# The order of loads and of seven hidden products in the spectral stage, and where the right sums are made, in a two-layer FNet and spatial-shift MLP kernel

## The chip, the cores and the metric

The kernel runs on one core of one Trainium2 chip. TensorE multiplies, VectorE (DVE) and ScalarE (ACT) prepare its operands and take its results, GpSimd (POOL) does little, and SyncE (SP) issues nearly all DMA transfers. Each engine works off its own list of instructions in order; a semaphore joins them where one needs the other's result. The metric is the time of one execution on the device in microseconds (us), lower is better.

## The reference, cut to what matters

Two layers, each made of a Fourier mixing stage A and a spatial-shift MLP stage B, with S = 2048 rows and D = 512 columns, F = 1376, all float32.

```python
def A(x):                       # FNet mixing, on the normed x
    a = x @ dft_hid_re.T        # hidden DFT
    b = x @ dft_hid_im.T
    return dft_seq_re @ a - dft_seq_im @ b      # DFT along the sequence, real part
def B(x):
    h = gelu(layernorm(x) @ w1)
    g = [the four column quarters of h, shifted by +1, -1, +2, -2 rows]
    x1 = x + concat(g) @ w2
    return x1 + gelu(layernorm(x1) @ w3) @ w4
for layer in range(2):
    x = x + A(layernorm(x))
    x = x + B(layernorm(x))
```

## The kernel before, in words

**Three products for one.** Every float32 operand is split into a high part (a copy rounded to the type fp32r, made on ACT) and a low part (the difference, made on DVE). `mm3` (L328 to L330) then multiplies high by high, high by low and low by high. So before TensorE can use a block of data, ACT must have made its high part and, behind it, DVE its low part.

**The spectral stage of layer 1.** It works through four column blocks c of the sequence DFT. For each block there is an x-phase (`x_phase`) and a y-phase (`y_phase`). An x-phase has eight steps k of two half-steps each. The even half-step 2k multiplies a "plain" block into the PSUM banks psc and psb: 12 products of 512 columns. The odd half-step 2k+1 multiplies the "one" block, a difference of the plain block's two halves, into psa: 6 products. A y-phase also has eight steps, with blocks "by1" (into psc and psd) and "by0" (into psb and psa), 12 products each; these blocks are sums of two loaded pieces.

**The seven forms.** In the x-phases of blocks 1, 2 and 3 the hidden DFT of the block before is done as well. It is a product of 2×2 sub-blocks, made by a scheme of seven products ("forms") in place of eight. `hid7` issues form n: 24 products of 256 columns into the PSUM bank psd0 or psd1, by turns. The left factor is one of seven sums of the earlier block (`forms`); its high part goes into one of two tiles, `hf[n % 2]` (`form_high`, on ACT, L475), its low part to its place (`form_low`, on DVE, L479). The right factors, seven right sums of the hidden DFT matrix, are the same for all blocks. They lie in DRAM (`hsd`, seven tiles of two halves), already split, and are loaded as needed. `hid7_out` adds a form's PSUM bank into the result tiles (DVE, `add`, L552). The tuple `HAT7` says ahead of which half-step each form stands; the dictionary `late` says at which half-step each left sum, high part and low part is issued.

**Loads.** All blocks of the stage are one list of `pieces` of 512 KB. `issue_dma` issues them in the order of the list, each as soon as one of the raw buffers is free: there are four, and in these phases two more ("wide"), six in all. A raw buffer of a DFT block is free once its parts are made; that of a form's half once TensorE has used it. If the next piece finds no buffer, no later one is issued. `prefetch` makes the parts of coming blocks, up to the four tiles of the ring. A DMA shows as `raw<-in_ws` for a DFT block and as `rawr<-hsd` for half of a form's right factor.

**Where the right sums come from.** They are made once, in layer 0, during the last pair of MLP blocks (`by_pairs` with `next_too`). There TensorE runs over the MLP's hidden blocks in products of 512 columns. At 26 points of that loop a function `one()` pops one item off the list `bg` and issues it; an item is other background work (preparing the next layer's blocks). `hs_forms` makes the right sums in four quarters; `hs_quarter` gives each quarter's work: load m, load r (the imaginary and the real part of a piece of the hidden DFT matrix, 256 KB each), four sums on DVE, and for each of the seven results a high part (ACT), a low part (DVE) and a store to `hsd`. In the program before, a quarter's work is seven items, some of them merged by `do_both`, and stands over 23 of the points, each behind the point's own item. The MLP's own weights, `w3b` (1792 KB) and `w4r` (512 KB), are loaded by the same queue, SP's. The tiles `rest` hold the sums of the MLP's branches; DVE (`add`, L552) and ACT (L1303) take PSUM banks through them.

What else touches the x-phases of layer 1: `w4_sums` at half-steps 10 and 11 (four sums of 256 columns on DVE, a high and a low part), `y_stats` (the statistics of a normalization, BATCH_NORM on DVE), and loads of result tiles by `rows`.

Of the kernel before, what the change touches and what calls it, by code (L numbers as in the profile page):

```python
# [8 lines left out]
F32 = mybir.dt.float32  # L9
# [9 lines left out]
NP = NT // 2  # L19
# [21 lines left out]
HAT7 = (3, 5, 7, 9, 10, 12, 14)  # L41
# [3 lines left out]
def spectral_mlp_kernel(ctx: ExitStack, tc: tile.TileContext, x, ws, hs, w1, w2, w34, out):  # L45
# [123 lines left out]
    def form_items(step):  # L169
        for h in range(7):  # L170
            if HAT7[h] == step:
                for j in range(2):
                    item("form", piece(hsd[h][j]), dest=hsd)
                    y_pieces.add(len(pieces) - 1)

    for layer in range(LAYERS):
        for c in range(NC):
            if layer == 0 and c == 0:
                for k in range(NP):
                    item("plain", piece(ws[c, k][:, 2:4]))  # L180
                    item("plain", piece(ws[c, k][:, 0:2]))
                continue
            for k in range(NP):
                if c and layer:
                    form_items(2 * k)
                elif c:
# [5 lines left out]
                if c and layer:  # L192
                    y_pieces.add(p)
                    form_items(2 * k + 1)
# [364 lines left out]
    def x_phase(c, hook, seven=False, tiles=0):  # L559
# [13 lines left out]
        for k in range(NP):  # L573
# [15 lines left out]
            mm_half(PB, ax[k][:, 1], s[:, 1], first, last)  # L589
            if last:  # L590
# [4 lines left out]
            form_steps(2 * k + 1)  # L595
# [4 lines left out]
            mm_half(PA, ax[k][:, 0], s[:, 0], first, last)  # L600
        for i in range(2):
            nc.scalar.copy(re0s[:, i], PA[i])

    def y_phase(c, hook, tiles=0):
# [32 lines left out]
        if tiles:  # L637
            for i, f in (
                (0, form_sum(im1s, im1s, re1s)),
                (0, form_sum(im1s, im1s, X1, ALU.add)),  # L640
                (1, lambda: form_high(0)),
                (1, form_sum(s3[1], a11f, a21f)),
                (2, lambda: form_low(0)),
                (2, form_sum(re1s, re1s, t[:, 0:2], ALU.add)),
                (3, form_sum(re0s, re0s, t[:, 0:2], ALU.add)),
                (3, form_sum(re0s, re0s, t[:, 2:4], ALU.add)),
                (4, lambda: form_high(1)),
                (4, form_sum(s2[1], a22f, s3[1])),
                (4, form_sum(a21f, a21f, a22f, ALU.add)),
                (4, lambda: form_low(1)),  # L650
                (5, lambda: form_high(2)),
                (5, form_sum(a11f, a12f, s2[1])),
                (6, lambda: form_low(2)),
                (7, lambda: form_high(3)),
                (8, lambda: form_low(3)),
                (8, lambda: form_high(4)),
                (9, lambda: form_low(4)),
                (10, lambda: form_high(5)),
                (11, lambda: form_low(5)),
                (12, lambda: form_high(6)),  # L660
                (13, lambda: form_low(6)),
# [180 lines left out]
    def by_pairs(layer, zs, xin, dst):  # L842
# [261 lines left out]
        def do_both(f, g):  # L1104
            return lambda: (f(), g())
# [81 lines left out]
        def hs_quarter(m, r, fp, places):  # L1187
# [948 lines left out]
```

## Time and profile before

| | us |
|---|---|
| median of 3 runs | 1500.86 (1498.94 to 1501.42) |
| profiled execution, its own time | 1500.71 |
| its span, first to last instruction | 1498.6 |
| TensorE busy | 1436.8 |
| VectorE busy | 1205.8 |
| ScalarE busy | 733.4 |
| TensorE waits for low parts at L479 (s, reL, imL) | 39.2 |
| mean granted TensorE clock | 0.987 |

The span leaves out 2.1 us that lie around it. A row of a wait list reads: who waits, for whom and which line, total us, times, longest. A row of the timeline reads: start, length, engine, line, operation, output <- input, shapes, and in brackets how long the engine had idled and what released it; PE's products are pipelined, so the distance from one start to the next is the cost of one, not its length. A granted clock of 0.50 means that TensorE ran at half speed there.

### The profile page before, as it was taken

The page shows a single profiled execution, that of the slowest core. Times are in us where ns is not written, and L with a number is a line of the kernel's source. Part 1 is how long each engine was busy: PE and PEld are TensorE (multiplying, and loading weights), DVE is VectorE, ACT ScalarE, POOL GpSimd, SP SyncE. Part 2 cuts the span into 40 slices and gives each one's busy share as a digit, 9 for nine tenths or more (in the row PEclk, how much of TensorE's full clock was granted, in tenths as well). Part 3 has the DMA queues.
Part 4 walks back from the last instruction along what each step waited for, and adds up shares of the span by engine and source line. Part 5 has one row for each costly group of instructions (what it writes and reads, how often), then busy time and mean ns, then how long its engine had stood idle before and what let it go on. Part 6 is the DMA issues. An engine that isn't in the chain of part 4 may idle for free.

```text
span 1498.6 us, 18501 instructions
## 1 busy us (share of the span) xinstructions
PE 1436.8 (96%) x6681; PEld 1200.9 (80%) x6681; DVE 1205.8 (80%) x1725; ACT 733.4 (49%) x1020; POOL 74.5 (5%) x105
## 2 busy tenths in 40 slices
PE   9999999999999999988999789889879999999999
PEld 7888888888888888866788678678768888889887
DVE  7986988989878886667899679769759887897676
ACT  5664454545566554344464234334325676454342
POOL 2100000000011000000000000000000011000000
PEclk9999999999999999989999989999989999999999
DMA  7866658478537679666655666666667637587864
GB/s 250 275 207 230 190 169 278 156 256 278 180 115 216 233 260 346 234 235 208 233 197 181 197 192 216 196 200 222 197 219 221 195 118 245 172 256 224 322 188 171
DMA packets 145628, 325.24 MB, mean 217 GB/s; under 512 B 10624, under 2 KB 61568, under 8 KB 142848
## 3 DMA queue, kind: packets, MB, share of 16 engines
q1 hardware_dynamic: 145536, 324.05, 65.5%
q8 instruction: 53, 0.87, 0.2%
q14 instruction: 39, 0.32, 0.1%
HBM read 262.41 MB, written 61.60 MB: 216 GB/s over the span
## 4 chain that ended last, share of the span: by engine, by line
PE 81%; DVE 9%; DMA 5%; ACT 3%; issue 2%; SPq 0%; POOL 0%; DVEq 0%; ACTq 0%; POOLq 0%
PE psd L330 9%; PE psd L328 8%; PE psd L329 8%; PE psa L330 7%; PE psa L329 7%; PE psa L328 7%; PE psb L330 6%; PE psb L329 6%; PE psb L328 6%; PE psc L329 6%; PE psc L330 6%; PE psc L328 6%; DMA raw<-in_ws 3%; DVE ring L285 2%; DMA hsd<-hp 1%
## 5 line engine op out<-in xcount | busy, mean ns | idle before, releaser
L264 ACT CAST ring<-raw 128x1024 fp32r<-128x1024 f32 x103 | 107.9, 1051 | 108.6 <-DMA raw<-in_ws 48.5
L285 DVE TENSOR_TENSOR ring<-raw,ring 128x1024 fp32r<-128x1024 f32 x102 | 124.1, 1219 | 41.6 <-ACT ring L264 41.5
L271 ACT CAST ring<-ring0f 128x1024 fp32r<-128x1024 f32 x28 | 29.5, 1052 | 69.1 <-DVE ring0f L270 69.1
L368 POOL TENSOR_TENSOR rs<-ve,mhalf 128x4 f32<-128x4 f32 x16 | 24.0, 1501 | 786.2 <-DVE nm L367 786.2
L285 DVE TENSOR_TENSOR ring<-ring1f,ring 128x512 fp32r<-128x512 f32 (+1 forms) x56 | 53.3, 951 | 5.2 <-ACT ring L267 5.1
L328 PE MATMUL psd<-rawr,hf 128*128 128x256 f32 x168 | 53.1, 316 | 3.6 <-ACT hf L475 3.6
L329 PE MATMUL psd<-rawr,hf 128*128 128x256 f32 x168 | 52.2, 310 | 0.0
L285 DVE TENSOR_TENSOR ring<-ring3f,ring 128x1024 fp32r<-128x1024 f32 (+1 forms) x50 | 49.2, 984 | 2.8 <-ACT ring L267 2.4
L328 PE MATMUL psd<-ring,ay 128*128 128x512 f32 x126 | 49.2, 391 | 1.9 <-DVE tmp L552 1.9
L347 POOL TENSOR_TENSOR rs<-ve,mhalf 128x2 f32<-128x2 f32 (+2 forms) x33 | 29.4, 889 | 434.2 <-DVE nb L346 415.2
L376 ACT ACTIVATE tmp<-xs,nb,rs 128x512 f32<-128x512 f32 x56 | 43.3, 810 | 14.5 <-POOL nb L348 13.0
L329 PE MATMUL psb<-ring,ay 128*128 128x512 f32 x128 | 49.9, 390 | 0.0
L328 PE MATMUL psb<-ring,ay 128*128 128x512 f32 x128 | 49.8, 389 | 0.0
L328 PE MATMUL psc<-ring,ay 128*128 128x512 f32 x128 | 49.8, 389 | 0.0
L330 PE MATMUL psb<-ring,ay 128*128 128x512 f32 x128 | 49.8, 389 | 0.0
L330 PE MATMUL psc<-ring,ay 128*128 128x512 f32 x128 | 49.8, 389 | 0.0
L329 PE MATMUL psc<-ring,ay 128*128 128x512 f32 x128 | 49.8, 389 | 0.0
L330 PE MATMUL psd<-ring,ay 128*128 128x512 f32 x126 | 49.0, 389 | 0.0
L328 PE MATMUL psa<-ring,ay 128*128 128x512 f32 x126 | 49.0, 389 | 0.0
L330 PE MATMUL psa<-ring,ay 128*128 128x512 f32 x126 | 49.0, 389 | 0.0
L329 PE MATMUL psa<-ring,ay 128*128 128x512 f32 x126 | 49.0, 389 | 0.0
L329 PE MATMUL psd<-ring,ay 128*128 128x512 f32 x126 | 49.0, 389 | 0.0
(898 smaller groups left out, 4766.9 us busy)
## 6 DMA issues: line engine op xcount, KB each, us to landing
raw<-in_ws SPq DMA_DIRECT2D x183, 512.0 KB, 5.0
w4r<-w4d SPq DMA_DIRECT2D x44, 512.0 KB, 4.7
rawr<-hsd SPq DMA_DIRECT2D x42, 512.0 KB, 4.1
w3b<-w3d SPq DMA_DIRECT2D x10, 1792.0 KB, 9.4
raw<-in_hs SPq DMA_DIRECT2D x32, 512.0 KB, 3.9
w3d<-w3b SPq DMA_DIRECT2D x5, 1792.0 KB, 6.9
hsd<-hp SPq DMA_DIRECT2D x28, 256.0 KB, 2.8
x1d<-tmp SPq DMA_DIRECT2D x12, 512.0 KB, 6.8
```

The costliest lines, as they stand in the source:

```text
L264: nc.scalar.copy(dest[:, a:b, 0], r[0][:, a:b])
L271: nc.scalar.copy(dest[:, :, 0], lo)
L285: nc.vector.tensor_tensor(lo, src, hi.bitcast(F32), op=ALU.subtract)
L328: nc.tensor.matmul(o, lh, rh, start=first, stop=False, skip_group_check=more)
L329: nc.tensor.matmul(o, lh, rl, start=False, stop=False, skip_group_check=more)
L330: nc.tensor.matmul(o, ll, rh, start=False, stop=last, skip_group_check=more)
L347: nc.gpsimd.tensor_tensor(rs[:, :n], ve[:, :n], mhalf[:, 0, :n], op=ALU.pow)
L368: nc.gpsimd.tensor_tensor(rs, ve, mhalf[:, :, :2], op=ALU.pow)
L376: nc.scalar.activation(o, s, AF.Identity, bias=mr[2], scale=mr[1])
```

## The change

Nothing is computed differently; the same products, sums and loads stand in another order. Four things are changed.

1. **Loads of an x-phase and its y-phase.** For blocks 1 to 3 of layer 1, a new function `ahead_pieces` lists all pieces of both phases with a due time in half-steps: a DFT block of x at 2k − 4.5, a form's halves one half-step before its place, a piece of y at 16 + 2k − 3.5. The list is sorted by due time and issued in that order. The items (the order in which blocks are used) take their pieces from it by name. All of these pieces may use the wide buffers.
2. **Places of the forms.** `HAT7` goes from (3, 5, 7, 9, 10, 12, 14) to (5, 10, 11, 12, 13, 14, 15), and the `late` list of sums, highs and lows is dealt out anew. The x-phase's last copies of PSUM banks stand behind the form of half-step 15, and `form_outs(2 * NP)` behind the last half-step issues what outs are left.
3. **Small moves in the x-phases.** `w4_sums` goes from half-steps 10 and 11 to 13 and 15, and a load of `pairs[1]` from 5 to 7.
4. **The right sums.** A quarter has five parts: the four sums; results 3, 4, 2; results 0, 1; result 6; result 5. They stand at 20 points, five for each quarter. In a point, the highs stand ahead of the point's own item and the lows and stores behind it. The next quarter's loads of m and r stand behind the fourth and the fifth point. The tiles lie at other places, so that the loads do not overwrite what is still in use.

```diff
-HAT7 = (3, 5, 7, 9, 10, 12, 14)
+XLEAD, YLEAD = 4.5, 3.5
+HAT7 = (5, 10, 11, 12, 13, 14, 15)
...
-    def form_items(step):
+    def ahead_pieces(c):
+        order = [(2 * k - XLEAD, 0, (k,), ws[c, k][:, 2:4]) for k in range(NP)]
+        order += [(t - 1, j, (h, j), hsd[h][j]) for h, t in enumerate(HAT7) for j in range(2)]
+        for k in range(NP):
+            order += [(2 * NP + 2 * k - YLEAD, i, (k, "y", i), ws[c, k][:, 2 - 2 * i : 4 - 2 * i]) for i in range(2)]
+        order.sort(key=lambda o: o[:2])
+        ids = {name: piece(src) for _, _, name, src in order}
+        y_pieces.update(ids.values())
+        return ids
+
+    def form_items(step, ids):
         for h in range(7):
             if HAT7[h] == step:
                 for j in range(2):
-                    item("form", piece(hsd[h][j]), dest=hsd)
-                    y_pieces.add(len(pieces) - 1)
+                    item("form", ids[h, j], dest=hsd)
 
     for layer in range(LAYERS):
         for c in range(NC):
...
+            if c and layer:
+                ids = ahead_pieces(c)
+                for k in range(NP):
+                    form_items(2 * k, ids)
+                    item("plain", ids[(k,)])
+                    form_items(2 * k + 1, ids)
+                    item("one", ids[(k,)], span=(0, 1))
+                for k, kind in y_order():
+                    item(kind, ids[k, "y", 0], ids[k, "y", 1])
+                continue
             for k in range(NP):
-                if c and layer:
-                    form_items(2 * k)
-                elif c:
+                if c:
                     for h in range(NP):
                         if HAT[h] == k:
                             item("plain", piece(hs[HORDER[h % 4]]))
                 p = piece(ws[c, k][:, 2:4])
                 item("plain", p)
-                if c and layer:
-                    y_pieces.add(p)
...
             form_outs(2 * k)
             mm_half(PC, ax[k][:, 2], s[:, 0], first, last)
             mm_half(PB, ax[k][:, 1], s[:, 1], first, last)
+            form_steps(2 * k + 1)
             if last:
                 for i in range(2):
                     nc.scalar.copy(im1s[:, i], PC[i])
                 for i in range(2):
                     nc.scalar.copy(re1s[:, i], PB[i])
-            form_steps(2 * k + 1)
             s = stream()
             run_late(2 * k + 1)
             hook(2 * k + 1)
             form_outs(2 * k + 1)
             mm_half(PA, ax[k][:, 0], s[:, 0], first, last)
+        form_outs(2 * NP)
         for i in range(2):
             nc.scalar.copy(re0s[:, i], PA[i])
 
...
             for i, f in (
                 (0, form_sum(im1s, im1s, re1s)),
-                (0, form_sum(im1s, im1s, X1, ALU.add)),
-                (1, lambda: form_high(0)),
-                (1, form_sum(s3[1], a11f, a21f)),
-                (2, lambda: form_low(0)),
-                (2, form_sum(re1s, re1s, t[:, 0:2], ALU.add)),
...
-                (8, lambda: form_low(3)),
-                (8, lambda: form_high(4)),
-                (9, lambda: form_low(4)),
-                (10, lambda: form_high(5)),
-                (11, lambda: form_low(5)),
-                (12, lambda: form_high(6)),
-                (13, lambda: form_low(6)),
+                (1, form_sum(im1s, im1s, X1, ALU.add)),
+                (2, lambda: form_high(0)),
+                (2, form_sum(s3[1], a11f, a21f)),
...
+                (6, form_sum(re0s, re0s, t[:, 2:4], ALU.add)),
+                (7, lambda: form_high(1)),
+                (7, form_sum(s2[1], a22f, s3[1])),
+                (8, lambda: form_high(2)),
+                (8, form_sum(a21f, a21f, a22f, ALU.add)),
+                (8, lambda: form_low(1)),
+                (9, form_sum(a11f, a12f, s2[1])),
+                (9, lambda: form_low(2)),
+                (10, lambda: form_high(3)),
+                (11, lambda: form_low(3)),
+                (11, lambda: form_high(4)),
+                (12, lambda: form_low(4)),
+                (12, lambda: form_high(5)),
+                (13, lambda: form_low(5)),
+                (13, lambda: form_high(6)),
+                (14, lambda: form_low(6)),
...
                 d, v = n // 2, slice(n % 2, n % 2 + 1)
-                m, r = (at(f"hs{i}{n}", STG + word, 1, CH, dtype=F32) for i, word in (("m", CH), ("r", 0)))
-                fp = [both(f"hp{i}{n}", RAWS + i * CH + CH, 1, 2, DH) for i in range(3)]
+                m, r = (at(f"hs{i}{n}", RAWS + (1 + i) * CH, 1, CH, dtype=F32) for i in range(2))
+                fp = [both(f"hp{i}{n}", word, 1, 2, DH) for i, word in enumerate((RAWS + 3 * CH, STG, STG + CH))]
                 steps += hs_quarter(m, r, fp, [(t[d][:, v], hs[(1, d)][:, v], hs[(0, d)][:, v]) for t in hsd])
             return steps
...
             def load_r():
                 nc.sync.dma_start(r, places[0][2])
 
-            def out(i, n, src=None):
-                t, src = fp[i][0], raw[i] if src is None else src
-                act(t[:, :, 0], src)
-                nc.vector.tensor_tensor(t[:, :, 1], src, t[:, :, 0].bitcast(F32), op=ALU.subtract)
-                nc.sync.dma_start(places[n][0].rearrange("p i (l w) -> p i l w", l=2), t.bitcast(F32))
-
             def sums():
-                add(raw[0], b22, b12, ALU.subtract)
                 add(raw[1], b12, b11, ALU.subtract)
-                out(0, 4)
-
-            def more_sums():
-                add(raw[2], b22, raw[1], ALU.subtract)
-                add(b12, raw[2], b21, ALU.subtract)
-                out(1, 3)
-
-            return [
-                load_m,
-                load_r,
-                sums,
-                more_sums,
-                lambda: out(2, 2),
-                lambda: (out(0, 0, b11), out(1, 1, b12)),
-                lambda: (out(2, 6, b21), out(0, 5, b22)),
+                add(raw[2], b22, b12, ALU.subtract)
+                add(raw[0], b22, raw[1], ALU.subtract)
+                add(b12, raw[0], b21, ALU.subtract)
+
+            def outs(*which):
+                which = [(i, n, raw[i] if src is None else src) for i, n, src in which]
+
+                def highs_():
+                    for i, _, src in which:
+                        act(fp[i][0][:, :, 0], src)
+
+                def lows_():
+                    for i, n, src in which:
+                        t = fp[i][0]
+                        nc.vector.tensor_tensor(t[:, :, 1], src, t[:, :, 0].bitcast(F32), op=ALU.subtract)
+                        nc.sync.dma_start(places[n][0].rearrange("p i (l w) -> p i l w", l=2), t.bitcast(F32))
+
+                return highs_, lows_
+
+            nothing = lambda: None
+            parts = [
+                (nothing, sums),
+                outs((1, 3, None), (2, 4, None), (0, 2, None)),
+                outs((1, 0, b11), (2, 1, b12)),
+                outs((0, 6, b21)),
+                outs((1, 5, b22)),
             ]
+            return [(load_m, load_r), *parts]
 
         def next_block(c, half, to):
             return lambda: b_in(c, half, to)
...
                 hcs[8:] = [hx[:, 0], hx[:, 1], rest[0]]
-                for n in (4, 10, 16):
-                    work[n : n + 2] = [do_both(*work[n : n + 2])]
-                work[20:22] = [do_both(*work[20:22])]
                 bg += [lows("t4"), *early]
-                bg[: len(work)] = [do_both(*fg) for fg in zip(bg, work)]
+                for n in range(4):
+                    parts = work[6 * n + 1 : 6 * n + 6]
+                    for i, (before, behind) in enumerate(parts):
+                        more_ = []
+                        if n < 3 and i > 2:
+                            more_.append(work[6 * n + 6][i - 3])
+                        bg[5 * n + i] = do_all(before, bg[5 * n + i], behind, *more_)
...
             then = [[] for _ in range(NF + 2)]
             if pair == 0:
                 work = hs_forms()
-                then[9] = [work.pop(0), work.pop(0)]
+                then[9] = [*work[0]]
                 next_blocks((3, 1, "22"))
                 then[1] = [lambda: w3_load(NF // 2)]
                 then[2] = [lambda: rows(xs[0], dst, 0, 2, False)]
...
-        if i == 10:
+        if i == (13 if layer else 10):
...
-        if i == 11:
+        if i == (15 if layer else 11):
...
                 if layer:
                     if i == 1:
                         rows(X1, xin, j, 2, True)
-                    if i == 5:
+                    if i == 7:
                         rows(pairs[1], xin, j + 2, 2, True)
                     if i == 15 and c < NC - 1:
                         y_stats(j + 2, pairs[1])
```

The lists of the engines show it at three places. In these rows the first word is the line (the changed program's lines stand some 15 to 30 lower down), `raw` and `rawr` are raw buffers, `hsd_89` to `hsd_102` the halves of forms 0 to 6, two each.

SyncE, the loads around the forms of column block 1, before:

```order
L243 DMA raw_209<-in_ws 128x1024
L243 DMA rawr_216<-hsd_89 128x1024
L243 DMA rawr_217<-hsd_90 128x1024
L243 DMA raw_208<-in_ws 128x1024
L243 DMA rawr_218<-hsd_91 128x1024
L243 DMA rawr_219<-hsd_92 128x1024
L243 DMA raw_209<-in_ws 128x1024
L224 DMA tmp<-x2d 128x2x512
L243 DMA rawr_214<-hsd_93 128x1024
```

and in the changed program:

```order
L258 DMA raw_210<-in_ws 128x1024
L258 DMA raw_211<-in_ws 128x1024
L258 DMA raw_208<-in_ws 128x1024
L258 DMA rawr_218<-hsd_89 128x1024
L258 DMA rawr_219<-hsd_90 128x1024
L258 DMA raw_209<-in_ws 128x1024
L239 DMA tmp<-x2d 128x2x512
L258 DMA raw_210<-in_ws 128x1024
L1867 DMA w4sumf<-in_w 128x2x256 x2
L258 DMA rawr_217<-hsd_91 128x1024
L258 DMA rawr_218<-hsd_92 128x1024
```

Before, the halves of forms 0 and 1 alternate with DFT blocks; afterwards more DFT blocks stand ahead of form 0, and three more loads lie between it and form 1.

ScalarE in column block 1, the high parts from form 3's to form 6's (hf_190 and hf_191 are the two hf tiles), before:

```order
L475 CAST hf_191<-imLf 128x1024
L267 CAST ring_206<-ring3f 128x512
L475 CAST hf_190<-s3f 128x1024
L264 CAST ring_200<-raw_209 128x2x512
L267 CAST ring_202<-ring1f 128x512
L475 CAST hf_191<-imLf 128x1024
L1857 CAST w4sum<-w4sumf 128x4x256
L264 CAST ring_204<-raw_213 128x2x512
L267 CAST ring_206<-ring3f 128x512
L475 CAST hf_190<-reLf 128x1024
```

and in the changed program:

```order
L490 CAST hf_191<-imLf 128x1024
L282 CAST ring_202<-ring1f 128x512
L490 CAST hf_190<-s3f 128x1024
L490 CAST hf_191<-imLf 128x1024
L279 CAST ring_204<-raw_213 128x2x512
L490 CAST hf_190<-reLf 128x1024
L1881 CAST w4sum<-w4sumf 128x4x256
L282 CAST ring_206<-ring3f 128x512
```

The highs of forms 4 and 5 now follow each other, and the high of the last plain block (ring_204) stands right behind form 5's.

SyncE while the right sums are made, around the second quarter's loads, before (hsm and hsr are a quarter's m and r, hp the tiles of its results):

```order
L927 DMA w4r_249<-w4d_113 128x1024
L1201 DMA hsd_101<-hp_4390 128x512
L1201 DMA hsd_99<-hp_4386 128x512
L1192 DMA hsm_4392<-in_hs 128x512
L942 DMA w3b_238<-w3d_85 128x3584
L1195 DMA hsr_4393<-in_hs 128x512
L1201 DMA hsd_97<-hp_4394 128x512
```

and in the changed program, where both are named hs:

```order
L1230 DMA hsd_101<-hp_4386 128x512
L1208 DMA hs_4392<-in_hs 128x512
L943 DMA w4r_249<-w4d_113 128x1024
L1230 DMA hsd_99<-hp_4388 128x512
L1211 DMA hs_4393<-in_hs 128x512
L958 DMA w3b_238<-w3d_85 128x3584
L1230 DMA hsd_95<-hp_4396 128x512
```

The load of r now stands ahead of w3b's, and the load of m ahead of a w4r load.

More of the change, by code (lines that the diff above doesn't have):

```diff
@@ L191, in spectral_mlp_kernel @@
                 item("plain", p)
-                if c and layer:
-                    y_pieces.add(p)
-                    form_items(2 * k + 1)
                 item("one", p, span=(0, 1))
@@ L639, in y_phase @@
                 (0, form_sum(im1s, im1s, re1s)),
[L640 to L661 removed]
+                (1, form_sum(im1s, im1s, X1, ALU.add)),
+                (2, lambda: form_high(0)),
+                (2, form_sum(s3[1], a11f, a21f)),
+                (3, lambda: form_low(0)),
+                (4, form_sum(re1s, re1s, t[:, 0:2], ALU.add)),
+                (5, form_sum(re0s, re0s, t[:, 0:2], ALU.add)),
+                (6, form_sum(re0s, re0s, t[:, 2:4], ALU.add)),
[14 more added lines that the diff above has]
+                (14, lambda: form_low(6)),
             ):
@@ L1102, in one, with do_all @@
                 bg.pop(0)()
-        def do_both(f, g):
-            return lambda: (f(), g())
+        def do_all(*fs_):
+            return lambda: [f() for f in fs_]
         def do(*fks):
```

## The prediction

> **What bounds the kernel now.** I read the head of the page first.
>
> ```profile
> span 1498.6 us, 18501 instructions
> PE 1436.8 (96%) x6681; PEld 1200.9 (80%) x6681; DVE 1205.8 (80%) x1725; ACT 733.4 (49%) x1020; POOL 74.5 (5%) x105
> ```
>
> TensorE is busy for 1436.8 of 1498.6 us, so it idles for 61.8 us, and a change of order can win back little more than that, plus what the reduced clock behind the waits costs. The second view is what TensorE waited for (total us, times, longest).
>
> ```profile
> PE psd L330 <- DVE s L479: 14.2, 6, 5.1
> PE psd L330 <- DVE reL L479: 13.2, 6, 4.5
> PE psd L330 <- DVE imL L479: 11.8, 6, 2.9
> ...
> PE psa L328 <- DVE rest L552: 3.5, 2, 3.3
> ...
> PE psa L328 <- ACT rest L1303: 1.2, 1, 1.2
> ```
>
> The first three are the low parts of the forms, made on VectorE at L479: 39.2 us, all in the three x-phases of layer 1. The last two belong to the stage that makes the right sums. The third view is the windows: columns are length, busy time of PE, its weight loads, DVE, ACT and POOL with counts, granted clock, DMA share, GB/s.
>
> ```profile
> 817.80:893.20 75.40, 60.59 (x319) 52.18 (x317) 49.54 (x61) 25.38 (x32) 0.61 (x1) 0.93 0.60 196
> 935.50:1008.80 73.30, 59.55 (x320) 51.22 (x318) 49.60 (x61) 25.44 (x32) 0.68 (x1) 0.95 0.62 200
> 1051.10:1127.90 76.80, 60.71 (x320) 52.81 (x319) 48.49 (x54) 24.62 (x31) 0.00 (x0) 0.93 0.64 213
> 627.30:703.10 75.80, 66.07 (x265) 52.19 (x264) 51.03 (x106) 34.64 (x67) 2.78 (x6) 0.93 0.71 241
> ```
>
> The first three run from an x-phase's first product to the y-phase's first product into psd; the fourth is the four cycles in which the right sums are made. What they would take undisturbed comes from the timeline of column block 1:
>
> ```profile
> 817.81 0.39 PE L328 MATMUL psc<-ring,ax 128*128 128x512 f32 x1
> ...
> 820.53 0.39 PE L328 MATMUL psa<-ring,ax 128*128 128x512 f32 x1
> ...
> 872.95 0.28 PE L328 MATMUL psd<-rawr,hf 128*128 128x256 f32 x1
> ...
> 875.82 0.40 PE L328 MATMUL psc<-ring,ax 128*128 128x512 f32 x1
> ...
> 893.23 0.50 PE L328 MATMUL psd<-ring,ay 128*128 128x512 f32 x1 [0.94 <-DVE tmp L552]
> ```
>
> A plain half-step (12 products) is 820.53 − 817.81 = 2.72, so 0.2267 for a product of 512 columns; a step of both halves (18) is 4.08; a form (24 of 256 columns) is 2.87. Eight steps, seven forms and the six psc products of y's first half-step (1.36) make 8×4.08 + 7×2.87 + 1.36 = 54.1. Against 75.4, 73.3 and 76.8, less some hundredths at the windows' edges, the excess is 21.3, 19.1 and 22.7: 63.1 us in all, idle and half clock together. The fourth window holds 264 products, 59.8 us undisturbed: excess 16.0. These two places are all that the change touches with weight.
>
> **Why the forms are late.** Again block 1, before and around its forms, and the landing times of the loads (KB each, median us from issue to landing):
>
> ```profile
> 832.44 1.04 ACT L475 CAST hf<-reLf 128x1024 fp32r<-128x1024 f32 x1
> ...
> 834.20 1.22 DVE L479 TENSOR_TENSOR reL<-reLf,hf 128x1024 fp32r<-128x1024 f32 x1
> 835.35 0.68 DVE L552 TENSOR_TENSOR tmp<-tmp,psd 128x512 f32<-128x512 f32 x1
> 835.94 0.68 DVE L285 TENSOR_TENSOR ring<-ring3f,ring 128x512 fp32r<-128x512 f32 x1
> ...
> 844.61 0.33 SPq L243 DMA_DIRECT2D raw<-in_ws  x1
> ...
> 848.44 1.05 ACT L264 CAST ring<-raw 128x1024 fp32r<-128x1024 f32 x1 [7.24 <-DMA raw<-in_ws]
> 849.52 1.22 DVE L285 TENSOR_TENSOR ring<-raw,ring 128x1024 fp32r<-128x1024 f32 x1 [2.99 <-ACT ring L264]
> ...
> 865.46 1.55 DVE L552 TENSOR_TENSOR w4sumf<-w4sumf 128x256 f32<-128x256 f32 x4
> ...
> 890.74 1.28 DVE L362 BATCH_NORM_STATS2 st<-tmp 128x6 f32<-128x512 f32 x2
> 892.49 0.68 DVE L552 TENSOR_TENSOR tmp<-tmp,psd 128x512 f32<-128x512 f32 x1
> ```
>
> ```profile
> raw<-in_ws SPq DMA_DIRECT2D x13, 512.0 KB, 4.9
> rawr<-hsd SPq DMA_DIRECT2D x10, 512.0 KB, 4.0
> ```
>
> The X block loaded at 844.61 lands at about 848.4; ACT, whose list is in order, idles 7.24 us before its high part, and DVE 2.99 us before its low part, with the forms' parts queued behind on both. The load itself was issued late, because in the old list it stands behind forms' halves that occupy buffers. So the wait named "DVE low" is a chain of load, ACT and DVE. From the same rows, start to start: a low part of 1024 costs 1.15 (834.20 to 835.35, taken as 1.14), a 512-wide sum 0.6, the four w4 sums 1.5, statistics with their small followers 1.75 (890.74 to 892.49), a high 1.04.
>
> **The change in an x-phase.** Nothing is computed more or less. Loads are listed by due time, so X blocks no longer stand behind forms; form 0 stays early (half-step 5), and six forms stand at 10 to 15. I walk this from X0's first product at t = 0 with those durations.
>
> Form 0 is due at 3×2.72 + 2×1.36 = 10.9; its low is ready at 9.9. Form 1 is due at 23.3, its low at 23.9 by the listed sums: it waits 0.4 to 0.6. Forms 2 to 5 are due at 28.9 to 43.3 and in time: each has its low 2 us ahead or more. Their halves are in time as well, the tightest being form 5's second half (issued when form 4's first half frees a buffer, 4.2 us before need, against 4.0 landing), and those of forms 2 and 6 (5.6 us).
>
> Then a block on ACT: there are two hf tiles, so the high of form 5 cannot start until form 3 ends (36.4), and the high of the last X block stands behind it. It ends at 38.5, and DVE idles from 35.0 until then. From there DVE has two lows (2.28), w4 sums (1.5), the out of form 3 (0.6), X7's difference (0.6), Y0's two sums and two lows (4.56), X7's second low (0.6), form 6's low (1.14) and form 4's out, which is 1024 wide (1.14): 12.4 us, to 51.0. Form 6, due at 48.9, writes the psd bank that form 4's out empties: stall 2.2. Behind it DVE does Y1's sum, waits for its high and does the low (3.3), w4's low (1.14), the statistics (1.75) and the outs of forms 5 and 6 (1.2): with the release, 59.0. y's first psd product is due at 51.1 + 2.87 + 1.36 + 1.36 = 56.7 and waits 2.3.
>
> So excess 0.4 + 2.2 + 2.35 = 5.0 in blocks 1 and 2. In block 3 no statistics stand there (54 DVE instructions against 61 in the windows), but three more loads do; I take 3.3. Gains 63.1 − 13.3 = 49.8. Bounds: if the ACT block and the tail vanish in semaphore slack, excess 2 for a phase, gain 57; if every hop costs what it does in the row of 849.52, excess 12, gain 27. I take the walk, since all its durations are of rows. Moved at no cost: the w4 sums and rows of pairs[1], which stand in that walk; their cover is form 3 and 4 on TensorE, and uncovered they cost 1.5 once a phase. The outs added at the end of the x-phase carry nothing new.
>
> **The change in the right sums.** The old stage:
>
> ```profile
> 630.87 0.39 SPq L942 DMA_DIRECT2D w3b<-w3d  x1
> 631.31 0.42 SPq L1195 DMA_DIRECT2D hsr<-in_hs  x1
> ...
> 640.98 0.43 DVE L552 TENSOR_TENSOR hp01f<-hsr,hsm 128x256 f32<-128x256 f32 x1 [5.37 <-issue]
> ...
> 644.87 0.80 PE L328 MATMUL psa<-b,w3b 128*128 128x512 f32 x1 [3.30 <-DVE rest L552]
> ```
>
> ```profile
> w3b<-w3d SPq DMA_DIRECT2D x3, 1792.0 KB, 9.4
> ...
> hsm<-in_hs SPq DMA_DIRECT2D x3, 256.0 KB, 4.3
> hsr<-in_hs SPq DMA_DIRECT2D x3, 256.0 KB, 6.5
> ```
>
> The 256 KB hsr load is issued behind the 1792 KB one and lands after 6.5 us or more (631.31 to nearly 641 here); DVE stands before its first sum for 5.37, the eviction of "rest" is behind it, and TensorE waits 3.30, then runs at half clock. Afterwards this load stands ahead of w3b, so I give it hsm's 4.3. It is issued in a quarter's last point and used in the next quarter's first: points lie 59.8 / 20 = 2.99 apart, so it is late by 1.3 at each of three boundaries, 3.9. The three highs that now stand ahead of a point's own ACT work keep the 1.2 us wait for ACT: excess 5, gain 11. Bounds: all 16, or, if the next load's place behind a w4r load that waits for its second part on SP costs what w3b's does, 6.5 + 3.3 + 1.2, rounded to 12, gain 4.
>
> **The clock.** Waits of 2 us are partly followed by half clock (in the second fence the granted clock is the third number from the end):
>
> ```profile
> 882.43 0.39 PE L330 MATMUL psd<-rawr,reL 128*128 128x256 f32 x1 [2.10 <-DVE reL L479]
> ...
> 999.45 0.39 PE L330 MATMUL psd<-rawr,reL 128*128 128x256 f32 x1 [2.30 <-DVE reL L479]
> ```
>
> ```profile
> 883.00:886.30 3.30, 3.30 (x18) 3.30 (x17) 3.27 (x3) 1.04 (x1) 0.00 (x0) 0.50 0.32 63
> ...
> 998.50:1003.00 4.50, 3.55 (x26) 3.41 (x27) 4.46 (x5) 1.96 (x2) 0.00 (x0) 1.00 0.35 77
> ```
>
> After 2.10 us of waiting 3.3 us ran at 0.50, which costs 1.7; after 2.30 none did. My walk has five stalls of that size: 0 to 8.5, I take about one of them, +2. [...]
>
> **The sum.** It is made against the profiled execution's 1500.71 us (span 1498.6 and 2.1 around it), which is 0.15 under the median of 1500.86: 1500.7 − 49.8 − 11 + 2 = 1441.9, so 1442.
>
> **Rivals.** *A, the DVE–ACT alternation becomes the bound.* In the stretch of six forms each low needs a high before it. Between two forms and one step (9.82 us of TensorE) stand three pairs of high and low (about 2.5 each with their hop), the difference with its own pair (2.1) and two outs (1.2): 10.8 if nothing overlaps, 1 us more than TensorE takes, so 3 us over three such groups, and two more half-clock stretches (3.4): excess 11 instead of 5. DVE's share of 49.5 of 75.4 us speaks against it, the 2.99 in the row of 849.52 for it. Three phases at 11 give a gain of 30: 1500.7 − 30 − 11 = 1460. *B, the right sums keep their stalls*, because a quarter is as long a chain as a cycle (load, sums, three highs, lows, stores) and only the place of the wait moves: 1453. For it: the stage already holds DVE for 51 of 75.8 us. Against: the wait's longest single piece is the load's. *C, slower: the forms starve.* Six forms in a row ask for their halves faster than before. Three of them a phase have 5.6, 4.2 and 5.6 us, so at a landing of L the loss is 3 × (3L − 15.4); at the 9.4 us of the 1792 KB load it is 38 (1480), and it eats the whole gain at about 11.7. At 12.2 us the time is 1505. Against it: 4.0 and 4.9 in the rows, and a DMA share of 0.60 to 0.64 in these windows. *D, better*: all waits melt, excess 2 a phase and none in the right sums, 1500.7 − 57 − 16 = 1428.
>
> **How the numbers follow.** The forecast has 0.60, A 0.20, B 0.12, C 0.04, D 0.04. The forecast's own bounds and A together need 1427 to 1466: the lower end is D's, the upper A's with the half-clock term's upper part (+6). What a measurement can tell from no change is about 0.2%, 3 us. All cases but C are faster by far more: faster 0.95, same 0.01, slower 0.04.
>
> **What would show it.** Right: the wait list no longer has s, reL and imL at over 1 us each, the three windows shrink to 58 to 60 us, and in each a wait of about 2 us stands before form 6 (for the out of form 4) and before y's first psd product. The high of X7 starts on ACT right behind that of form 5, which starts at form 3's end. In the right sums the r load lands in about 4.3 us and the four cycles take about 65. Wrong: rawr landings of 8 us or more (C), many waits of about 1 us for L494 lows (A), the four cycles still above 72 (B), or half-clock stretches as many as now. A late load anywhere in the stretch of six forms would break the walk, since each stall there shifts every later due time.

## The result, and the profile after

The changed kernel takes 1455.25 us (median of 4 runs, 1454.63 to 1457.12) against 1500.09 before: ratio 0.9703, 95% interval 0.9686 to 0.972. The forecast was 1442 in a range of 1427 to 1466, so the direction and the range hold and the gain is 45 us instead of 59.

The head of the page after, to be read against that of before:

```profile
span 1452.9 us, 18506 instructions
...
PE 1420.9 (98%) x6681; PEld 1188.4 (82%) x6681; DVE 1204.9 (83%) x1725; ACT 731.8 (50%) x1020; POOL 76.6 (5%) x105
```

TensorE's idle time fell from 61.8 to 32.0 us, and its busy time by 15.9. A product at half clock counts as a longer one: the one of 512 columns at 872.64 is given 0.63 us, with the next start 0.43 later; at 649.42, at full clock, it is 0.39 and 0.23. Between 100 and 1420 us the clock records have 37.5 us at half clock before and 10.2 after. What TensorE waited for, over the whole run:

```profile
PE psd L343 <- DVE tmp L567: 7.8, 3, 3.2
PE psd L343 <- issue: 4.8, 3, 2.0
PE psa L343 <- DVE rest L567: 4.3, 3, 3.1
PE psd L343 <- DVE rest L567: 3.3, 2, 2.7
PE psc L343 <- ACT rr11f L608: 1.7, 1, 1.7
PE psd L345 <- DVE reL L494: 1.6, 3, 0.6
...
PE psd L343 <- DMA rawr<-hsd: 1.0, 1, 1.0
```

The 39.2 us for the forms' low parts are down to 1.6. New is the first row, y's first psd product behind the outs of forms 5 and 6, once in each of the three blocks; the second is form 6. The two rows for rest are the right sums. The same four stretches as windows (blocks 1, 2, 3, then a stretch of half clock, then the four cycles of the right sums):

```profile
810.40:871.60 61.20, 55.26 (x319) 47.99 (x317) 51.66 (x63) 24.93 (x32) 1.13 (x2) 1.00 0.68 230
915.40:976.50 61.10, 55.26 (x320) 47.99 (x318) 51.69 (x63) 24.93 (x32) 1.16 (x2) 1.00 0.69 231
1020.40:1081.30 60.90, 55.48 (x319) 47.91 (x318) 49.96 (x56) 24.94 (x32) 0.00 (x0) 1.00 0.71 247
...
871.40:874.70 3.30, 3.08 (x7) 2.48 (x8) 1.42 (x3) 1.05 (x1) 1.29 (x2) 0.50 0.99 258
...
627.80:698.30 70.50, 62.85 (x265) 50.28 (x264) 52.55 (x109) 34.59 (x66) 3.01 (x6) 0.98 0.72 253
```

They were 75.4, 73.3, 76.8 and 75.8. The row 871.40:874.70 is half clock just behind block 1's window. Since TensorE issues the same 6681 products, the start of the n-th product in both traces, taken where the order is the same in both, tells what was won up to there. So read, forecast and measurement stand like this:

| | forecast gain, us | measured, us |
|---|---|---|
| right sums | 11 | 8.0 |
| block 1 | 16.3 | 12.7 |
| block 2 | 14.1 | 10.5 |
| block 3 | 19.4 | 14.8 |
| half clock | −2 | in the rows above |
| sum | 58.8 | 46.0 |

The two spans differ by 45.7 us; the rows add up to a little more because the changed kernel was 0.5 us behind where the right sums begin.

### The profile page after: what moved, and what is told of

Read it like the earlier page. It is cut to its first block, busy times and chain, and to the rows that moved or that the text cites. A ratio compares the mean times of both kernels' runs of the same rounds, so it can differ in the third digit from the quotient of the medians.

```text
span 1452.9 us, 18506 instructions
## 1 busy us (share of the span) xinstructions
PE 1420.9 (98%) x6681; PEld 1188.4 (82%) x6681; DVE 1204.9 (83%) x1725; ACT 731.8 (50%) x1020; POOL 76.6 (5%) x105
## 4 chain that ended last, share of the span: by engine, by line
PE 83%; DVE 9%; DMA 4%; ACT 2%; issue 2%; SPq 0%; DVEq 0%; ACTq 0%
PE psd L343 8%; PE psd L345 8%; PE psd L344 8%; PE psa L343 7%; PE psa L344 7%; PE psa L345 7%; PE psb L344 6%; PE psb L343 6%; PE psb L345 6%; PE psc L344 6%; PE psc L345 6%; PE psc L343 6%; DVE ring L300 1%; DVE rest L567 1%; DMA raw<-in_ws 1%
## 5 line engine op out<-in xcount | busy, mean ns | idle before, releaser
L286 ACT CAST ring<-ring2f 128x1024 fp32r<-128x1024 f32 x28 | 29.6, 1056 | 48.8 <-DVE ring2f L285 48.8
L343 PE MATMUL psd<-rawr,hf 128*128 128x256 f32 x168 | 47.7, 284 | 5.8 <-issue 4.8
```

The costliest lines, as they stand in the source:

```text
L286: nc.scalar.copy(dest[:, :, 0], lo)
L343: nc.tensor.matmul(o, lh, rh, start=first, stop=False, skip_group_check=more)
```

## The experiments

**Which part wins.** The change was taken apart. `x_only` is the kernel before with parts 1 to 3 of the change, `sums_only` with part 4 alone.

> The kernel before with the x-phases' part alone (list of loads, places of the forms, dealt-out parts, small moves); the right sums stay as before. If the two parts do not touch each other, as the alignment of the two traces says (38 us won in the three x-phases, 8 in the right sums), this gives 1500.1 - 37 = 1463, within 2. Rival: the parts share SP's queue and VectorE, and one of them gives the other its gain: off 1463 by 4 us or more.

> The kernel before with the right sums at 20 points alone. By the alignment of the traces 8 us: 1492, within 2. Rival: the sums' new places win only because something else moved: 1500; or all 16 us of excess there were theirs: 1484.

Measured: x_only 1463.84 us (ratio 0.9755, 0.9728 to 0.9782), sums_only 1491.52 (0.9943, 0.9926 to 0.996), before 1500.92 on that chip. Both numbers are met, 37.1 and 9.4 us; their sum is the whole gain of 45 within the spread, so the two parts add up.

Then the x-phases' part was divided once more. `loads_only` has the list of loads by due time, with the forms and their parts where they were:

```diff
+XLEAD, YLEAD = 4.5, 3.5
 HAT7 = (3, 5, 7, 9, 10, 12, 14)
...
+            if c and layer:
+                ids = ahead_pieces(c)
...
```

> The kernel before with the list of loads by due time alone; the forms stay at half-steps 3, 5, 7, 9, 10, 12, 14 with their old list of parts. My theory: the late low parts are a chain that begins with loads stuck behind forms' halves, so this alone takes more than half of the 37 us: 1482 or less. Rival: the places of the forms and of their parts decide, and with forms every second half-step the low parts stay late whatever the loads do: 1493 to 1500.

`forms_only` has the forms and their parts at the new places and the small moves of part 3, with the old list of loads:

```diff
-HAT7 = (3, 5, 7, 9, 10, 12, 14)
+HAT7 = (5, 10, 11, 12, 13, 14, 15)
...
                 if c and layer:
                     form_items(2 * k)
...
```

> The kernel before with the new places of the forms and of their parts (and the small moves), the loads in their old order, in which a DFT block stands behind the halves of the forms used before it. My theory (loads are the first link): less than half of the 37 us, 1482 to 1500, with waits for forms' halves or blocks. Rival (places decide): 1463 to 1470.

Measured: loads_only 1462.84 us (0.9752, 0.9721 to 0.9784), as much as x_only; forms_only 1512.95 (1.009, 1.0055 to 1.0124), slower than before. ScalarE's waits show why, here for a block's high part (the same line under three numbers; total us, times, longest), first before, then forms_only; in loads_only and in the changed kernel a single one, of 0.4 us, is left in these phases.

```profile
ACT ring L264 <- DMA raw<-in_ws: 48.5, 12, 8.0
```

```profile
ACT ring L265 <- DMA raw<-in_ws: 39.5, 9, 8.2
```

Waits of TensorE in loads_only:

```profile
PE psd L345 <- DVE reL L494: 9.0, 6, 2.1
...
PE psd L345 <- DVE imL L494: 4.0, 5, 1.2
PE psd L343 <- ACT hf L490: 3.4, 3, 1.1
```

And in forms_only the waits, with form 5 of block 1 and what came before it:

```profile
PE psd L329 <- issue: 43.5, 9, 10.2
```

```profile
866.15 0.32 SPq L244 DMA_DIRECT2D rawr<-hsd  x1
...
866.58 13.72 SPq L244 DMA_DIRECT2D raw<-in_ws  x3
...
873.78 1.23 DVE L271 TENSOR_TENSOR ring0f<-raw,raw 128x1024 f32<-128x1024 f32 x1 [8.83 <-DMA raw<-in_ws]
...
878.13 0.68 DVE L553 TENSOR_TENSOR tmp<-tmp,psd 128x512 f32<-128x512 f32 x1
...
878.90 0.55 PE L329 MATMUL psd<-rawr,hf 128*128 128x256 f32 x1 [9.96 <-issue]
```

With the loads in due order the forms' waits for low parts fall from 39 us to 13 even at their old places: the late low part was the end of the chain load, ACT, DVE.

With the old loads and six forms in a row, twelve halves stand close together in the list, and the DFT blocks behind them come late. The row of 866.15 is the last of these halves, form 6's. Behind it the two pieces of y's first block are issued (866.58 and 867.59; the row merges them with the next), and VectorE idles 8.83 us for their sum. Behind that sum in its list stands the out of form 3 (878.13), which empties the bank that form 5 writes. It ends at 878.81, and form 5 starts after a wait of 9.96 us, which the profile can only call "issue". Form 5's own halves, issued at 852.0 and 852.4, had landed by 858.6. All nine waits of the row of 43.5 us end with such an out of a form's bank, and none with the landing of a half. So the first link is again a DFT block's load that stands behind forms' halves.

The new places (with the small moves) cost 12 us without the new loads, and on top of the new loads they are worth nothing (1463.84 against 1462.84). My theory held and was too cautious: the loads bring not more than half but all of it.

**The waits that are left in an x-phase.** Block 1 of the changed kernel, from form 5's high to y's first psd product, on DVE, ACT and PE:

```profile
847.35 1.05 ACT L490 CAST hf<-imLf 128x1024 fp32r<-128x1024 f32 x1 [3.15 <-PE psd L344]
848.30 1.04 ACT L279 CAST ring<-raw 128x1024 fp32r<-128x1024 f32 x1
849.37 1.23 DVE L300 TENSOR_TENSOR ring<-raw,ring 128x1024 fp32r<-128x1024 f32 x1 [3.33 <-ACT ring L279]
...
860.74 1.21 DVE L567 TENSOR_TENSOR tmp<-tmp,psd 128x1024 f32<-128x1024 f32 x1
...
862.05 0.36 PE L343 MATMUL psd<-rawr,hf 128*128 128x256 f32 x1 [2.00 <-issue]
...
863.87 1.23 DVE L285 TENSOR_TENSOR ring2f<-raw,raw 128x1024 f32<-128x1024 f32 x1 [1.92 <-DMA raw<-in_ws]
...
867.41 1.22 DVE L1883 TENSOR_TENSOR w4sum<-w4sumf,w4sum 128x1024 fp32r<-128x1024 f32 x1
868.55 1.28 DVE L377 BATCH_NORM_STATS2 st<-tmp 128x6 f32<-128x512 f32 x2
...
870.29 1.28 DVE L567 TENSOR_TENSOR tmp<-tmp,psd 128x512 f32<-128x512 f32 x2
...
871.62 0.80 PE L343 MATMUL psd<-ring,ay 128*128 128x512 f32 x1 [3.19 <-DVE tmp L567]
```

The block on ACT is there as forecast: form 5's high waits for form 3, the last plain block's high stands behind it, DVE idles 3.33. What the forecast did not have is at 863.87: the sum of y's second step waits 1.92 us for its load (3.36 in block 3), and w4's low, the statistics and the outs of forms 5 and 6 are behind it. The first of its two pieces stands in the list behind form 6's second half, which got a buffer of form 5's only at 855.9; the second piece was issued at 857.4, when the second sum of y's first step had freed its buffer, and landed after 6.4 us. The edit against the first of these moves one high by a half-step, `high5_behind`:

```diff
-                (12, lambda: form_high(5)),
+                (13, lambda: form_high(5)),
```

> The changed kernel, with the high part of form 5 issued one half-step later, behind the high part of the last plain block instead of ahead of it. Theory: VectorE's idle stretch of 3.3 us shrinks and the wait of 2.0 us before form 6 goes, but the sum of y's second step waits for a load that lands at the same time as before, and the outs of forms 5 and 6 stand behind it: the wait before y's first psd product grows by what was won. 1455, within 1.5. Rival (the forecast's, in which VectorE's list alone sets both waits): 2.0 + 2.0 + 0.8 won in the three blocks, 1450.

The edit against the second, `outs_first`, holds back the staging of y's second step and puts w4's low, the statistics and the outs ahead of it:

```diff
+            held_back = last and seven
+            if held_back:
+                limit, state["limit"] = state["limit"], state["one"]
             form_steps(2 * k + 1)
+            if held_back:
+                issue_dma()
+                state["limit"] = limit
+                hook(2 * k + 1)
+                form_outs(2 * NP)
...
```

> The changed kernel, with w4's low part, the statistics and the outs of forms 5 and 6 put ahead of the sum of y's second step on VectorE (that block is staged one half-step later). Theory: the wait before y's first psd product (3.2, 3.2, 1.5 us) comes from the load wait (1.9, 1.9, 3.4 us) in front of the outs; it goes, and with it the two half-clock stretches (1.7 each): 1455 - 7.9 - 3.4 = 1444. Rival: VectorE has no time to spare there, and the wait comes back one step later, at y's second step: 1452 to 1456.

> Both edits of the two kernels high5_behind and outs_first. Theory: with the load wait out of the way, the 2.0, 2.0 and 0.8 us before form 6 are won as well: 1444 - 4.8 = 1439. Rival: the form's own chain sets that wait, so 1444.

Measured: high5_behind 1453.47 us (0.9686, 0.9659 to 0.9713), outs_first 1441.16 (0.9608, 0.9575 to 0.964), outs_high5 1441.54 (0.9606, 0.958 to 0.9632). In outs_first the whole row "psd <- DVE tmp" is gone, and the granted clock is 1.00 from 810 to 890 us and 0.999 over the whole run (0.996 in the changed kernel):

```profile
PE psd L343 <- issue: 4.6, 3, 2.0
PE psa L343 <- DVE rest L567: 3.9, 3, 2.8
PE psd L343 <- DVE rest L567: 3.0, 2, 2.3
PE psd L345 <- DVE reL L494: 1.6, 3, 0.6
```

So the outs stood behind a load, and it cost 14 us, 3 more than I counted; two waits of block 3 that I had not counted, 1.7 us for a copy on ACT and 1.0 for a right factor, are gone as well, but a part of the 3 us stays unexplained. The other two went differently from my reason. high5_behind came within 1.6 us of the time I expected, and outs_high5 is no faster than outs_first (I expected 5 us): form 6's wait was not shortened at all in either of them. The trace of outs_high5 shows where it went:

```profile
843.77 1.05 ACT L279 CAST ring<-raw 128x1024 fp32r<-128x1024 f32 x1
...
852.64 1.05 ACT L490 CAST hf<-reLf 128x1024 fp32r<-128x1024 f32 x1 [4.57 <-PE psd L344]
853.60 1.04 ACT L1889 CAST w4sum<-w4sumf 128x1024 fp32r<-128x1024 f32 x1
854.54 0.61 ACT L282 CAST ring<-ring3f 128x512 fp32r<-128x512 f32 x1
855.19 0.69 DVE L300 TENSOR_TENSOR ring<-ring3f,ring 128x512 fp32r<-128x512 f32 x1 [2.06 <-ACT ring L282]
```

The plain block's high now runs at 843.77 instead of 848.30, but form 6's high waits for the other hf tile until form 4 ends at 852.6, and the next block's high is behind that one: the same block, one form later. `hf_w4` therefore moves form 6's high as well, and w4's sums off that stretch:

```diff
                 form_outs(2 * NP)
+                hook(2 * NP)
...
-                (13, lambda: form_high(6)),
+                (14, lambda: form_high(6)),
...
-        if i == (13 if layer else 10):
+        if i == (15 if layer else 10):
...
-        if i == (15 if layer else 11):
+        if i == (16 if layer else 11):
```

> The kernel outs_high5 with form 6's high put behind the highs of the last step's blocks, and with w4's sums put behind form 4's out and their low part behind the outs of forms 5 and 6. Theory: in outs_high5 the block on ScalarE (a high that waits for one of two hf tiles, with a block's high behind it) only moved from form 5's high to form 6's, where VectorE idles 2.1 us; without it, and with 1.5 us of w4's sums moved, form 4's out ends before form 6 is due, and its wait (2.0, 2.0, 0.6 us) goes: 1441 - 4.6 = 1436.5. Rival: form 6's wait is for the landing of its right factor, not for the out: 1441.

Measured: 1439.52 us (0.9572, 0.955 to 0.9594) on a chip where before took 1504.72. Against outs_high5's ratio of 0.9606 that is 5 us of 1500, but the intervals overlap and the times themselves, from two chips, differ by only 2.0, so the size of this gain stays open. Form 6 in block 1:

```profile
858.53 1.21 DVE L567 TENSOR_TENSOR tmp<-tmp,psd 128x1024 f32<-128x1024 f32 x1
859.84 0.36 PE L343 MATMUL psd<-rawr,hf 128*128 128x256 f32 x1 [0.41 <-issue]
```

Form 4's out starts 1.9 us earlier than in outs_high5 (860.42 there) and form 6 follows its end: its wait is 0.41 instead of 2.00, so the out, not the landing of the right factor, was what it waited for. In block 3, however, a y product then waits 2.2 us for a block's low part, so not all of it is kept.

**The right sums.** One boundary of two quarters in the changed kernel:

```profile
648.09 0.47 SPq L1211 DMA_DIRECT2D hs<-in_hs  x1
648.66 0.44 SPq L958 DMA_DIRECT2D w3b<-w3d  x1
653.82 0.43 DVE L567 TENSOR_TENSOR hp12f<-hs 128x256 f32<-128x256 f32 x1 [3.72 <-DMA hsd<-hp]
...
661.48 0.50 PE L343 MATMUL psa<-b,w3b 128*128 128x512 f32 x1 [3.05 <-DVE rest L567]
```

r is issued ahead of w3b now, but w3b follows 0.6 us behind, and the second sum, the first to need r, starts at 654.34: r landed 6.2 us after its issue, not 4.3 (4.9 and 5.8 at the other two boundaries). VectorE idles 3.72, TensorE's wait for rest is 3.05. The releaser that the profile names is the store of result 5, whose tile the first sum writes. `swap56` separates the two:

```diff
-                outs((0, 6, b21)),
-                outs((1, 5, b22)),
+                outs((1, 6, b21)),
+                outs((0, 5, b22)),
```

> The changed kernel, with results 6 and 5 of the right sums in each other's tile, so that the next quarter's first sum writes a tile whose store was issued a point earlier. VectorE idles 3.7 and 3.3 us there, and the trace names the store of result 5. Theory: the load of r, issued after that store, lands at the same time (the second sum starts 0.2 us behind its landing), so the wait only moves from the first sum to the second: 1455, within 1. Rival: the store's tile is the cause: 2 to 3 us at each of three boundaries, 1447 to 1449.

Measured: 1456.00 us (0.9702, 0.9675 to 0.973), no change; now each sum waits for the load it needs, 1.23 for m and 2.12 for r:

```profile
650.48 0.42 DVE L567 TENSOR_TENSOR hp12f<-hs 128x256 f32<-128x256 f32 x1 [1.23 <-DMA hs<-in_hs]
653.02 0.42 DVE L567 TENSOR_TENSOR hp22f<-hs,hs 128x256 f32<-128x256 f32 x1 [2.12 <-DMA hs<-in_hs]
```

`r_earlier` then issues both loads a point earlier, by making results 6 and 5 in one point:

```diff
-                outs((0, 6, b21)),
-                outs((1, 5, b22)),
+                outs((0, 6, b21), (1, 5, b22)),
+                (nothing, nothing),
...
-                        if n < 3 and i > 2:
-                            more_.append(work[6 * n + 6][i - 3])
+                        if n < 3 and 1 < i < 4:
+                            more_.append(work[6 * n + 6][i - 2])
```

> The changed kernel, with results 6 and 5 of the right sums both made in a quarter's fourth point, so that the next quarter's loads of m and r are issued one point (3 us) earlier each; the fifth point holds no work of the sums. Theory: VectorE's idle 3.7 and 3.3 us before a quarter's first sums is the landing of r (6.1 us from issue, with w3b issued just behind it), so it shrinks by about 3 us at each of three boundaries, and TensorE's waits for rest there (7.6 us in all) and one half-clock stretch (1.7) mostly go: 1455 - 6 = 1449, within 2. Rival: a quarter is too long a chain for a cycle whatever the load does (two highs and lows more stand in one point), the wait only moves: 1454 to 1457.

Measured: 1448.54 us (0.9635, 0.9609 to 0.9661). The four cycles take 64.2 us against 70.5, the clock stays full:

```profile
627.20:691.40 64.20, 60.98 (x265) 49.21 (x264) 52.32 (x109) 34.27 (x66) 3.01 (x6) 1.00 0.75 274
```

So the landing of these two loads was what the stage waited for, and a quarter is not too long a chain for a cycle, as rival B had it.

**Both together.**

> The edits of r_earlier and of hf_w4 in one kernel. Theory: they are at different places and add up: 1436.5 - 6 = 1430.5. Rival: neither acts: 1441.

Measured: 1431.21 us (0.9518, 0.9496 to 0.954), below both kernels of the case. TensorE is busy 99% of its span, and the longest waits left are these:

```profile
PE psd L343 <- DVE rest L567: 2.6, 3, 1.4
PE psd L345 <- DVE reL L494: 1.6, 3, 0.6
PE psb L344 <- DVE ring L300: 1.6, 1, 1.6
PE psd L343 <- issue: 1.4, 3, 0.6
```

What wasn't tried: a third hf tile, which would take away the block on ACT at its root, and the old places of the forms with equally good placing of what follows them. Whether six forms in a row are needed for 1431 stays open.

## Why the prediction was right, and where it was not

**The cause** was right: the forms' low parts end a chain that begins with a DFT block's load that stands behind forms' halves. loads_only shows it by itself. The prediction priced the list of loads and the forms' new places as one edit and so did not see that all of the gain is the list's, and that the new places without it cost 12 us. Rival C, starvation of six forms in a row, happened only once in the changed kernel (a wait of 1.0 us in block 3, for a half that landed after 7.8), and it is not what makes forms_only slow: there the halves had landed, and the forms waited for outs that stood behind late DFT blocks on VectorE.

**The walk** was right up to form 6: form 1 waits 0.5 to 0.6 in each block (0.4 to 0.6 forecast); VectorE idles 3.33 behind the block on ACT (3.5); form 6 waits 2.00, 2.00 and 0.80 (2.2 forecast).

**The step that failed in the x-phases** is the last one, "Behind it DVE does Y1's sum, waits for its high and does the low (3.3)". It took Y1's pieces as landed. They are issued behind form 6's halves, which themselves wait for a buffer of form 5's, and cost VectorE 1.92 us (1.80 in block 2, 3.36 in block 3). y's psd product so waits 3.19 and 3.18 instead of 2.3, and in block 3 two waits, 1.67 and 1.45, take the place of one. The excess up to that product is 7.1, 7.0 and 6.8 us instead of 5.0, 5.0 and 3.3: 7.6 of the missing 13. Not all of it is this step. In blocks 1 and 2 the wait before y's psd product accounts for about 1.0 of the 2.1 us; the rest lies at form 1 and at y's first psc product, some 0.4 to 0.5 us each beyond the forecast, and in small delays. In block 3 the 1.0 us for a right factor is in it.

**The half clock** was put at about one stretch. Three came: behind both 3.2 us waits, at 871.4 and 977.2, and in the right sums at 680.2 behind a wait of 2.67; 3.41 us at 0.50 and so 1.7 us each, 5.1 instead of 2.

**The right sums** gave 8.0 instead of 11: 5.3 in the four cycles and 2.7 just behind them, where the forecast had nothing and where two waits for hidden blocks h (0.7 and 1.2 us before) are gone. The step is "so I give it hsm's 4.3"; r landed after 4.9, 6.2 and 5.8 us, so it was late by 1.9 to 3.2 us at a boundary rather than 1.3. (The lower bound of that gain rounds 6.5 + 3.3 + 1.2, which is 11.0, to 12; nothing else hangs on it.) The end of the wait, on the eviction into rest, was placed rightly.

**The rivals.** A (ACT and VectorE alternating as the bound, 1460) is near the measured time by number but not by mechanism: VectorE's share of a window is higher than before (51.7 of 61.2), yet moving the outs and the statistics ahead of one load, with no less work, won 14 us. B's time (1453) was nearer still, but the right sums kept 10.7 of their 16.0 us of excess, not all, and most of the miss lies in the x-phases.

## What to carry to other kernels

When a wait names a vector operation, follow it back to what that operation's engine stood waiting for, and try the first link alone: here, in the x-phases, the order of the loads was the whole effect. After such a repair walk the lists of every in-order engine past the repaired place and ask for each instruction that waits for a load what stands behind it; work that is already possible, here the outs of two forms, belongs ahead of it. A load's landing time is to be taken from a row of the queue it will have, with the large transfer that is issued behind it: here r, with 1792 KB issued 0.5 to 0.6 us behind it, took 4.9 to 6.2 us where 4.3 was assumed.

## What was not expected of the hardware

- A 256 KB load (r) issued 0.5 to 0.6 us ahead of a 1792 KB one landed after 4.9, 6.2 and 5.8 us in the changed kernel. Before, the one issued 0.4 us behind such a load (631.31) landed after 9.6 us, and those issued 5.9 and 11.5 us behind one after 6.5 and 4.2; the 6.5 that stands in the list of loads is the median of these three unlike cases. So r landed 3.4 to 4.7 us sooner just ahead of the large load than just behind it, but took longer than the median of 4.3 that the forecast gave it.
- Half clock did not go by the length of a wait alone. In the changed kernel it followed waits of 3.19, 3.18 and 2.67 us, and did not follow one of 3.05 (the row of 661.48) nor those of 2.00, 2.00 and 0.80; before, it followed one of 2.10 and not one of 2.30. The clock records in the traces of before and of the changed kernel show where the difference lies. In each of them all changes of the clock (19 before, 7 in the changed kernel) lie a whole number of steps of 3.413 us apart: in the changed kernel the clock falls at 680.21, 871.36 and 977.17, which are 56 and 31 steps from one to the next. Between 100 and 1420 us and by the ends of products that the profile models, the clock fell at the end of each of the 12 steps at full clock in which TensorE idled for 2.00 us or more, and at the end of none of the 745 others, which all had 1.90 or less. The waits of 2.67 and 2.10 us have 2.54 and 2.10 in one step; that of 3.05 is split into 1.3 and 1.7, and that of 2.30 into 1.8 and 0.5. So in these two traces the waits of 2 to 3 us were followed by a half-clock stretch or not by where they lay on these steps.
